# Output projection of tiles 0 to 7 in four pairs: seven products of halves and sums of halves, the fifth block of channels in plain products

## The chip, the core and the metric

The kernel runs on one core of a Trainium2 chip. The metric is the device time of one execution in microseconds, the median of several runs; lower is better. Five engines work side by side, each in its own program order: TensorE (PE, and PEld for its weight loads), VectorE (DVE), ScalarE (ACT), GpSimd (POOL) and SyncE (SP), which issues the DMAs here.

## The reference

A sequence of 2048 rows with 640 channels is normalized, goes through a sliding local attention with dilation (32 heads of 20 channels, 8 places at distance 2) and its output projection, and is gated by a bilinear feed-forward layer with 1536 hidden features:

```python
xn = _layernorm(x, axis=-1)
s = _A_ref(xn, A_wqkv, A_wo)             # attention, then @ wo
g = _silu(_B_ref(xn, B_w_gate, B_w_up, B_w_down))   # ((xn Wg) * (xn Wu)) Wd
return x + s * g
```

All matrix products have float32 inputs. The part that matters here is the last step of the attention, `o @ wo`: 2048 x 640 times 640 x 640.

## The kernel before

The 2048 rows lie in 16 tiles of 128. A product with float32 accuracy is made of three matmuls on TensorE: every operand is split into a high part `hi`, a copy on ScalarE in the type that TensorE multiplies quickly, and a low part `lo`, the operand less `hi`, made on VectorE or GpSimd (`split`, L83). `mm3` (L90) runs hi by hi over all blocks, then hi by lo, then lo by hi, into one PSUM bank.

The program runs in stages. The projections to queries, keys and values and the gate and up products (`gate_up`, L391) fill TensorE for the first 559 us, while VectorE does the attention (`attention`, L310) in small steps that `advance` and `drain` hand out. Each feature block `f` of the gate and up products runs over four chunks of 512 rows; the last two blocks are `f0` and `f1`. Then comes the output projection, 16 tiles of two column halves with 15 matmuls of 128x320 each (`out_proj`, L484), and at last the down products (`product`, L603).

The down products already use the scheme that the change brings to the output projection: two tiles make a pair, and the four quarters of the two-by-two product come out of seven products instead of eight (`W_IN`, `H_IN`, L497), with sums and differences of quarters as inputs. Three PSUM banks A, B, C serve them in the order A C A C A B A: a product with an old place accumulates on what the earlier one left, which ScalarE or VectorE must have read first (`gather`, L616). Quarter inputs for it are made ahead: `sum_wd` and `split_wd` (L517, L530) prepare the down weights during the output projection, one half block per tile.

Per tile the output projection takes these steps: `load_o` (L463) gathers the attention output from DRAM by four DMAs; `trans_o` (L472) turns the tile on VectorE in blocks of 32 by 32, copies `hi` on ScalarE and takes `lo` on VectorE; `out_proj` runs the 30 matmuls, and ScalarE copies each half to SBUF; one DMA stores the tile to `s_scr`. The tile of step s+1 is turned ahead of the matmuls of step s. The weight `wo` has five blocks of 128 channels, loaded and split behind the gate and up products (L775 to L788).

The order of each engine's work is the order of the program text. SBUF buffers go by tags with a fixed count of buffers (`st`, L75): a tile gets a buffer when the last reader of an earlier tile has finished. The tags of interest are `t` (two raw attention tiles of three), `wraw` (three raw weights), `wf` (four), `xc` (four: the normalized input, later down weights), `kv` (two: keys and values, later down weights) and `ot` (two turned tiles).

Of the kernel before, what the change touches and what calls it, by code (L numbers as in the profile page):

```python
# [19 lines left out]
P = 128  # L20
# [17 lines left out]
SCALE = DH ** -0.5  # L38
MASKED = -1e9 / SCALE
EPS = 1e-5  # L40
PAIRS = range(0, W, 2)
PACE = 1.0

# [7 lines left out]
def kernel(  # L51
# [23 lines left out]
    def st(shape, tag, bufs, dt=F32):  # L75
        cnt[0] += 1
        return sb.tile(shape, dt, tag=tag, bufs=bufs, name=f"{tag}_{cnt[0]}")

    def pt(shape, tag, bufs):
        cnt[0] += 1  # L80
        return ps.tile(shape, F32, tag=tag, bufs=bufs, name=f"{tag}_{cnt[0]}")

    def split(eng, raw, hi, lo):  # L83

        nc.scalar.activation(hi, raw, AF.Copy)  # L85
        eng.tensor_sub(lo, raw, hi.bitcast(F32))  # L86
# [3 lines left out]
    def mm3(acc, pairs, parts=ALL3, first=True, last=True):  # L90

        pairs = list(pairs)
        runs = [(a[i], b[j]) for i, j in parts for a, b in pairs]
        for n, (a, b) in enumerate(runs):
            nc.tensor.matmul(acc, a, b, start=first and n == 0, stop=last and n == len(runs) - 1)  # L95
# [376 lines left out]
    def trans_o(s):  # L472
        y = st([P, KD, P], "ot", 2)
        nc.vector.transpose(y.rearrange("p k (q i) -> p k q i", i=QB),
                            o_t.pop(s).rearrange("p (q k j) -> p k q j", q=NQ, j=QB))
        if s == NT - 2:
# [7 lines left out]
    def out_proj(s):  # L484
        a = oT.pop(s)
        y = st([P, D], "hs" if s % 2 and s < NT - 4 else "gs", 2)
        for n in range(2):
            c = slice(n * HALF, (n + 1) * HALF)
            p = pt([P, HALF], "q", 4)
            mm3(p, [([t[:, k, :] for t in a], [t[:, c] for t in wo_s[k]]) for k in range(KD)])  # L490
            nc.scalar.activation(y[:, c], p, AF.Copy)
        nc.sync.dma_start(s_scr[s], y)


    KH = KF // 2
# [4 lines left out]
    def begin_wd():  # L500

        big = [st([P, KH + 2, 2, HALF], "xc", NCH, F32R) for _ in range(4)]
        for name, y in zip(("B11", "T1", "T2", "B21"), big):
            wd_t[name] = [y[:, k] for k in range(KH)]
        wd_t["T3"] = [big[k // 2][:, KH + k % 2] for k in range(KH)]
        for name in ("B22", "T4"):
            y = st([P, KH, 2, HALF], "kv", 2, F32R)
            wd_t[name] = [y[:, k] for k in range(KH)]

    def load_wd(k):  # L510
        wd_raw[k] = st([P, 2, 2, HALF], "wraw", 3)
        for a in range(2):
            nc.sync.dma_start(wd_raw[k][:, a].rearrange("p a c -> p (a c)"), wd[:, a * KH + k, :])
# [126 lines left out]
        return lambda: None  # L640


    begin_unit(0)
    mask = st([1, NE, W], "mask", 1)
    nc.gpsimd.memset(mask, 0.0)
# [119 lines left out]
    for u in range(2, len(UN)):  # L765
        unit(u)
        for _ in range(3 + (u in (2, 5)) if u + 1 < len(UN) else len(pieces)):
            if len(pieces) == 1:
                load_wf(f1)
            piece()  # L770
    for ch in range(NCH):
        gate_up(f0, ch)
        if ch == 0:
            split_wf(f1, nc.gpsimd)
            load_wo((0, 1))  # L775
            load_wo((2, 3))
            t = load_wo((4,))
    for ch in range(NCH):
        if ch == 3:
            load_wd(0)  # L780
            trans_o(0)
            load_o(1, 1, st([P, 1, D], "o", 1))
            load_o(2, 3, st([P, 3, D], "t", 2))
            load_o(5, 3, st([P, 3, D], "t", 2))
        gate_up(f1, ch)
        if ch < 3:
            for k in ((0, 1), (2, 3), (4,))[ch]:
                split_wo(k)  # L788
        if ch == 1:
            drain(len(UN) - 2)  # L790
            load_o(0, 1, t[:, 1:2])
        if ch == 2:
            advance(1e9)

    load_wd(1)
    o_next = {3: (8, 3), 6: (11, 3), 9: (14, 2)}
    n_prod = 7 * NT // 2
    for s in range(NT):
        k, part = divmod(s - 1, 2)
        if s == 1:  # L800
            begin_wd()
        if s + 1 < NT:
            trans_o(s + 1)
        if s in o_next:
            load_o(*o_next[s], st([P, o_next[s][1], D], "t", 2))
        if 0 <= k < KH:
            sum_wd(k, part)
        out_proj(s)
        if 0 <= k < KH:
            split_wd(k, part)  # L810
            if part and k + 2 < KH:
                load_wd(k + 2)
        if s == 12:
            load_h(0)
        if s == 14:
            hi_h(0)
            lo_h(0)
# [72 lines left out]
```

## Time and profile before

| what | us |
|---|---|
| runs | 784.98, 783.54, 783.24 (median 783.54) |
| profiled execution | 783.21 |
| its span, first to last instruction | 781.4 |
| TensorE busy | 774.3 (99%) |
| VectorE busy | 667.2 (85%) |
| ScalarE busy | 230.9 (30%) |
| GpSimd busy | 135.8 (17%) |
| granted TensorE clock, mean | 0.999 |

The profile is that of one execution. Busy time is the time in which an engine has an instruction in work; matmuls are pipelined, so start-to-start distances say more of TensorE than durations. The "chain that ended last" follows the last instruction back to what released it, step by step. In groups and timelines the name left of the arrow is the tile that is written, those right of it are read; a group's row ends with the idle time of the engine ahead of its instructions and what ended it.

### The profile page before, as it was taken

Reading aid. Unit: us, or ns where it says so; the run is one execution under the profiler, and the core shown is the slowest. Engines: PE = TensorE matmul, PEld = TensorE weight load, DVE = VectorE, ACT = ScalarE, POOL = GpSimd, SP = SyncE. Lnnn points to the kernel's source line nnn. Section 1 sums busy time; section 2 is a strip of 40 time slices with the busy share of each in tenths; the row PEclk is TensorE's granted clock in tenths of the full one; section 3 lists DMA queues with packets and bytes.
Section 4 is the critical chain, followed back from the end, with each engine's and each line's share of the span. In section 5 each row is a group of like instructions: output and inputs, shape, how many; then the busy total and the mean of one; then the engine's idle time right before and its main releaser. Section 6 shows DMA issues by size and latency. Waiting matters only on the chain.

```text
span 781.4 us, 11205 instructions
## 1 busy us (share of the span) xinstructions
PE 774.3 (99%) x4432; PEld 706.1 (90%) x4432; DVE 667.2 (85%) x691; ACT 230.9 (30%) x527; POOL 135.8 (17%) x110
## 2 busy tenths in 40 slices
PE   8999999999999999999999999999999999999997
PEld 6989888898988898989898989888899999999997
DVE  6999898999999999996999998995368677777775
ACT  4323312031112121312131212112256554444442
POOL 5200401022013101210204001023177600000000
PEclk9999999999999999999999999999999999999999
DMA  9562131331224122423133131432967574555534
GB/s 330 161 198 75 43 96 38 96 90 48 84 49 124 49 64 81 119 61 79 29 99 92 39 105 39 129 100 70 242 186 217 167 263 156 198 192 183 182 101 136
DMA packets 82237, 93.99 MB, mean 120 GB/s; under 512 B 23096, under 2 KB 63368, under 8 KB 82056
## 3 DMA queue, kind: packets, MB, share of 16 engines
q1 hardware_dynamic: 82184, 93.27, 39.3%
q8 instruction: 35, 0.57, 0.3%
q14 instruction: 18, 0.15, 0.1%
HBM read 55.84 MB, written 28.31 MB: 108 GB/s over the span
## 4 chain that ended last, share of the span: by engine, by line
PE 99%; ACT 0%; DVE 0%; issue 0%; POOL 0%; POOLq 0%
PE q L299 27%; PE g L95 22%; PE u L95 22%; PE q L613 11%; PE q L95 9%; PE u L613 5%; PE g L613 3%; PE q L157 1%; PE q L223 0%; ACT xc L224 0%; PE g L223 0%; DVE q L599 0%; DVE q L600 0%; ACT q L594 0%; PE u L223 0%
## 5 line engine op out<-in xcount | busy, mean ns | idle before, releaser
L95 PE MATMUL g<-xc,wf 128*128 128x512 f32 (+1 forms) x735 | 176.4, 390 | 0.0
L95 PE MATMUL u<-xc,wf 128*128 128x512 f32 (+1 forms) x735 | 176.1, 390 | 0.0
L95 PEld LDWEIGHTS u<-xc,wf 128*128 128x128 f32 x735 | 135.7, 188 | 32.1
L95 PEld LDWEIGHTS g<-xc,wf 128*128 128x128 f32 x735 | 135.4, 188 | 31.1
L299 PE MATMUL q<-wqh,xc 128*128 128x300 f32 (+1 forms) x960 | 160.0, 310 | 0.9 <-ACT xc L224 0.9
L299 PEld LDWEIGHTS q<-wqh,xc 128*128 128x128 f32 x960 | 146.3, 188 | 2.8 <-ACT xc L224 1.3
L333 DVE TENSOR_TENSOR t<-q,kv 128x1600 f32<-128x1600 f32 (+1 forms) x48 | 96.9, 2018 | 9.1 <-DMA kv<-kv 9.1
L354 DVE TENSOR_TENSOR t<-e,kv 128x1600 f32<-128x1600 f32 (+1 forms) x48 | 97.6, 2050 | 1.1
L86 POOL TENSOR_TENSOR wf<-wraw,wf 128x256 fp32r<-128x256 f32 (+2 forms) x22 | 44.9, 2058 | 281.1 <-ACT wf L85 281.1
L336 DVE TENSOR_REDUCE lg<-t 128x80 f32<-128x1600 f32 (+1 forms) x48 | 92.6, 1929 | 1.1
L402 ACT ACTIVATE gs<-g 128x512 f32<-128x512 f32 x48 | 28.7, 597 | 213.9 <-PE g L95 208.7
L299 PE MATMUL q<-wql,xc 128*128 128x300 f32 (+1 forms) x480 | 86.2, 309 | 0.0
L301 ACT ACTIVATE kv<-q 128x200 f32<-128x200 f32 (+1 forms) x96 | 33.3, 347 | 144.9 <-PE q L299 144.9
L362 DVE TENSOR_TENSOR t<-t,t 128x1600 f32<-128x1600 f32 (+1 forms) x36 | 75.2, 2089 | 1.0
L299 PEld LDWEIGHTS q<-wql,xc 128*128 128x128 f32 x480 | 74.9, 188 | 0.0
L613 PE MATMUL q<-xc,wf 128*128 128x320 f32 x432 | 67.2, 308 | 0.0
L86 POOL TENSOR_TENSOR wql<-wraw,wqh 128x300 fp32r<-128x300 f32 (+4 forms) x15 | 36.1, 2431 | 168.3 <-ACT wqh L85 168.3
L613 PEld LDWEIGHTS q<-xc,wf 128*128 128x128 f32 x432 | 64.3, 188 | 0.0
L413 DVE TENSOR_TENSOR hs<-u,gs 128x512 f32<-128x512 f32 x47 | 32.1, 682 | 10.4 <-PE u L95 9.5
L95 PE MATMUL q<-wf,wf 128*128 128x320 f32 x156 | 35.1, 305 | 0.0
L86 DVE TENSOR_TENSOR wf<-ot,wf 128x640 fp32r<-128x640 f32 x13 | 15.0, 1156 | 20.0 <-ACT wf L85 17.1
L95 PEld LDWEIGHTS q<-wf,wf 128*128 128x128 f32 x156 | 26.0, 188 | 0.0
(170 smaller groups left out, 879.2 us busy)
## 6 DMA issues: line engine op xcount, KB each, us to landing
h_scr<-hs SPq DMA_DIRECT2D x48, 256.0 KB, 2.3
wraw<-in_wgu SPq DMA_DIRECT2D x12, 640.0 KB, 4.7
t<-h_scr SPq DMA_DIRECT2D x8, 768.0 KB, 7.8
hs<-s_scr SPq DMA_DIRECT2D x16, 320.0 KB, 3.9
gs<-in_x SPq DMA_DIRECT2D x16, 320.0 KB, 4.3
wraw<-h_scr SPq DMA_DIRECT2D x12, 384.0 KB, 6.2
out<-q SPq DMA_DIRECT2D x14, 320.0 KB, 2.6
wraw<-in_wd SPq DMA_DIRECT2D x12, 320.0 KB, 4.1
```

Source lines behind the costliest of these rows:

```text
L86: eng.tensor_sub(lo, raw, hi.bitcast(F32))
L95: nc.tensor.matmul(acc, a, b, start=first and n == 0, stop=last and n == len(runs) - 1)
L157: nc.tensor.matmul(pt([P, 3, P], "q", 4), ident, ident.unsqueeze(1).to_broadcast([P, 3, P]), start=True, stop=True)
L299: nc.tensor.matmul(p, xT[(r * NE + i) // TPC][a][:, k, t0:t0 + P], wq[g][b][:, k], start=n == 0, stop=n == len(runs) - 1, skip_group_check ...
L301: nc.scalar.activation(kv_t[u][:, :, W - 1 + i, :], p[:, c:].rearrange("p (a c) -> p a c", a=2), AF.Copy)
L333: nc.vector.tensor_mul(t, q.rearrange("p i c -> p (i c)").unsqueeze(1).to_broadcast([P, 2, NE * c]), places(0, j))
L336: nc.vector.tensor_reduce(out=lg[:, :, j:j + 2].rearrange("p n a -> p a n"), in_=heads(t), op=ALU.add, axis=AX.X)
L354: nc.vector.tensor_mul(heads(t), pw, heads(places(1, j)))
L362: nc.vector.tensor_add(acc, acc, t)
L402: nc.scalar.activation(gs, pp[0], AF.Copy)
L413: nc.vector.tensor_mul(hs, pp[1], gs)
L613: nc.tensor.matmul(p, y[:, i, k], wd_t[name][k][:, l], start=new and r == 0, stop=r == len(runs) - 1, skip_group_check=True)
```

## The change

Tiles 0 to 7 are taken in four pairs. With channels 0 to 255 and 256 to 511 as the two halves of the contraction and the two halves of the columns, each pair's quarters come out of seven products of two blocks each (six matmuls); the fifth block, channels 512 to 639, is added in plain products of three matmuls to the products that finish a quarter. Tiles 8 to 15 go as before.

What comes with it: the sums of quarters of `wo` are taken in place in its raw tiles and split into four more weights, held in parts of the `xc` buffers that the down weights fill later; the fifth block's difference of halves is one more. Each pair is loaded as one, turned, its sums taken (four on VectorE), and split in two parts of 768 and 1280 elements (`hi_pair` on ScalarE, `lo_pair` on VectorE) into parts of the `kv` and `xc` buffers or `wf`. The attention's remaining steps are handed out after the first chunk of `f1` instead of the third, the weights of blocks 2 and 3 are split a stage earlier, and the down weights are prepared at one half block per pair for the first three pairs, two for the fourth, then one per tile. The output tiles `y` are written by VectorE's additions as well as by ScalarE's copies.

```diff
     def trans_o(s):
-        y = st([P, KD, P], "ot", 2)
+        y = st([P, 2, KD, P], "ot", 2)[:, 0]
+        turn(y, s)
...
-            tag, n = ("kv", 2) if s == 0 else ("wf", 4) if s < NT - 2 else ("t", 2)
-            z = st([P, 2, KD, P], tag, n, F32R)
+            if s == SP:
+                z = blocks(wd_kv[0], 4, 2, KD)
...
+    def sums_wo():
+
+        r, u = wo_keep
+        b11, b12, b21, b22 = r[:, :, :HALF], r[:, :, HALF:], u[:, :, :HALF], u[:, :, HALF:]
+        nc.vector.tensor_sub(b11, b12, b11)
+        nc.vector.tensor_sub(b12, b22, b12)
+        nc.vector.tensor_sub(b22, b22, b11)
+        nc.vector.tensor_sub(b21, b21, b22)
+        wo_keep.append({"T1": b11, "T3": b12, "T2": b22, "T4": b21})
...
+    def split_t(name, y, r):
+        v = wo_keep[2][name]
+        t = y[:, r:r + KS]
+        split(nc.gpsimd, v, t[:, :, 0], t[:, :, 1])
+        wo_t[name] = [t[:, k] for k in range(KS)]
...
+    def load_pair(p):
+        t = st([P, 3, D], "t", 2)
+        load_o(2 * p, 2, t[:, 0:2])
...
+    def turn_pair(p):
+        y = pair_y[p] = st([P, 2, KD, P], "ot", 2)
+        for i in range(2):
+            turn(y[:, i], 2 * p + i)
+        s1, s2, s4 = (pair_raw[p][:, i] for i in range(3))
+        a11, a12, a21, a22 = (y[:, i, k:k + KS] for i in range(2) for k in (0, KS))
+        nc.vector.tensor_add(s1, a21, a22)
+        nc.vector.tensor_sub(s2, s1, a11)
+        nc.vector.tensor_sub(s4, a12, s2)
+        nc.vector.tensor_sub(a21, a11, a21)
+
+    def hi_pair(p, part):
...
+        nc.scalar.activation(z[0], raw, AF.Copy)
+
+    def lo_pair(p, part):
+        z, raw = pair_z[p, part]
+        nc.vector.tensor_sub(z[1], raw, z[0].bitcast(F32))
...
+    FIFTH = {3: ("a5", HALF), 4: ("b5", HALF), 5: ("a5", 0), 6: ("b5", None)}
+
+    def pair_product(p, j):
+        place = "ACACABA"[j]
+        new = j in (0, 1, 5)
...
+        runs = [(pair_in(p, H_IN[j], k, i), w_part(W_IN[j], k, l)) for i, l in ALL3 for k in range(KS)]
+        if j in FIFTH:
+            name, c = FIFTH[j]
+            runs += [(pair_in(p, name, 0, i), wo_t["W0-W1"][:, l] if c is None else wo_s[KD - 1][l][:, c:c + HALF])
+                     for i, l in ALL3]
...
+        kept, (ya, yb) = pair_k[0], y_t.setdefault((p, "y"), [None, None])
+        if j < 3:
+            nc.scalar.activation(kept[:, j], b, AF.Copy)
+        elif j == 3:
+            ya = y_t[p, "y"][0] = st([P, D], "gs", 2)
+            nc.vector.tensor_add(ya[:, HALF:], kept[:, 2], b)
+        elif j == 4:
+            yb = y_t[p, "y"][1] = st([P, D], "hs", 2)
+            nc.vector.tensor_add(yb[:, HALF:], kept[:, 1], b)
+        elif j == 5:
+            nc.vector.tensor_add(ya[:, :HALF], kept[:, 0], b)
+            nc.sync.dma_start(s_scr[2 * p], ya)
+        else:
+            nc.scalar.activation(yb[:, :HALF], b, AF.Copy)
+            nc.sync.dma_start(s_scr[2 * p + 1], yb)
...
+        elif ch < 3:
+            split_wo(ch + 1)
+    gate_up(f1, 0)
+    advance(1e9)
+    split_wo(0)
+    split_wo(1)
+    load_pair(0)
+    load_pair(1)
+    begin_wd(kv=True)
+    begin_wd()
+    gate_up(f1, 1)
+    split_wo(4)
+    sums_wo()
+    wo_keep.append(w5)
+    split_t("T1", wd_big[0], 4)
+    split_t("T2", wd_big[0], 6)
+    turn_pair(0)
+    hi_pair(0, 0)
+    hi_pair(0, 1)
+    begin_wd()
+    gate_up(f1, 2)
+    sum_w5()
+    split_w5()
+    lo_pair(0, 0)
+    lo_pair(0, 1)
+    split_t("T3", wd_big[1], 4)
+    split_t("T4", wd_big[1], 6)
+    load_pair(2)
+    load_wd(0)
     load_wd(1)
...
+    turn_pair(1)
+    begin_wd()
+    gate_up(f1, 3)
+    begin_wd()
+    hi_pair(1, 0)
+    sum_wd(0, 0)
+    split_wd(0, 0)
+    turn_pair(2)
...
+    pair_product(0, 0)
+    for p in range(SP // 2):
+        more = p + 1 < SP // 2
+        n = 1 + (p > 2)
+        if more:
+            lo_pair(p + 1, 0)
+        pair_product(p, 1)
+        wd_sums(n)
+        pair_product(p, 2)
+        if more:
+            hi_pair(p + 1, 1)
+        pair_product(p, 3)
+        wd_splits(n)
+        pair_product(p, 4)
+        if more:
+            lo_pair(p + 1, 1)
+        else:
+            trans_o(SP)
+        pair_product(p, 5)
+        if p == 0:
+            load_pair(3)
+        elif p == 1:
+            turn_pair(3)
+            load_o(SP, 3, st([P, 3, D], "t", 2))
+        elif p == 2:
+            load_o(SP + 3, 3, st([P, 3, D], "t", 2))
+        if more:
+            pair_product(p + 1, 0)
+        else:
+            out_proj(SP, 0)
+        pair_product(p, 6)
+        if p + 2 < SP // 2:
+            hi_pair(p + 2, 0)
```

`turn` is the transpose that stood in `trans_o`, `blocks` a view of a part of a buffer as operand blocks, and `wd_sums` and `wd_splits` walk through the half blocks of the down weights; `begin_wd` gives out its buffers one at a time.

More of the change, by code (lines that the diff above doesn't have):

```diff
@@ L498, with begin_wd, blocks @@
     H_IN = ("A11", "S1", "S2", "S4", "S3", "A12", "A22")
[L500 to L508, printed above, removed]
+    wd_big, wd_kv = [], []
+    def begin_wd(kv=False):
+        if kv:
+            for name in ("B22", "T4"):
+                y = st([P, KH, 2, HALF], "kv", 2, F32R)
+                wd_kv.append(y)
+                wd_t[name] = [y[:, k] for k in range(KH)]
+            return
+        y = st([P, KH + 2, 2, HALF], "xc", NCH, F32R)
+        wd_t[("B11", "T1", "T2", "B21")[len(wd_big)]] = [y[:, k] for k in range(KH)]
+        wd_big.append(y)
+        if len(wd_big) == NCH:
+            wd_t["T3"] = [wd_big[b][:, k] for b, k in ((2, 6), (2, 7), (3, 7), (3, 6), (1, 6), (1, 7))]
+    def blocks(y, r, h, n):
+        return y[:, r:].rearrange("p r i c -> p (r i c)")[:, :h * n * P].rearrange("p (h n c) -> p h n c", h=h, c=P)
     def load_wd(k):
@@ new lines, in split_t, with split_w5, w_part @@
+    def split_t(name, y, r):
[3 more added lines that the diff above has]
+        wo_t[name] = [t[:, k] for k in range(KS)]
+    def split_w5():
+        t = wd_kv[1][:, KH - 1]
+        split(nc.gpsimd, wo_keep[3][:, :HALF], t[:, 0], t[:, 1])
+        wo_t["W0-W1"] = t
+    def w_part(name, k, l):
+        if name in wo_t:
+            return wo_t[name][k][:, l]
+        a, c = divmod(int(name[1:]) - 11, 10)
+        return wo_s[a * KS + k][l][:, c * HALF:(c + 1) * HALF]
@@ new lines, in hi_pair @@
+    def hi_pair(p, part):
+        if part == 0:
+            if p % 2:
+                z = [st([P, 2, KD, P], "wf", 4, F32R).rearrange("p a k c -> p (a k) c")[:, :3 * KS] for _ in range(2)]
+            else:
+                z = blocks(wd_kv[1], 2, 2, 3 * KS)
+                z = [z[:, 0], z[:, 1]]
+            raw = pair_raw[p].rearrange("p a k c -> p (a k) c")
+        else:
+            z = blocks(wd_big[3], 3, 2, 2 * KD) if p % 2 else blocks(wd_kv[0], 2, 2, 2 * KD)
+            z = [z[:, 0], z[:, 1]]
+            raw = pair_y[p].rearrange("p a k c -> p (a k) c")
+        pair_z[p, part] = z, raw
+        nc.scalar.activation(z[0], raw, AF.Copy)
@@ L812 @@
                 load_wd(k + 2)
+        del wd_steps[:n]
+    pair_product(0, 0)
[14 more added lines that the diff above has]
+            lo_pair(p + 1, 1)
+        else:
+            trans_o(SP)
[9 more added lines that the diff above has]
+            pair_product(p + 1, 0)
+        else:
+            out_proj(SP, 0)
+        pair_product(p, 6)
+        if p + 2 < SP // 2:
+            hi_pair(p + 2, 0)
+    n_prod = 7 * NT // 2
+    for s in range(SP, NT):
+        if s + 1 < NT:
+            trans_o(s + 1)
+        if s == SP + 2:
+            load_o(SP + 6, 2, st([P, 2, D], "t", 2))
+        wd_sums(1)
+        if s > SP:
+            out_proj(s, 0)
+        out_proj(s, 1)
+        wd_splits(1)
         if s == 12:
```

84 lines of the change are left out of this document (42 added, 42 removed).

## The prediction

> **What bounds the kernel now.** I read the page first: the span, the chain that ended last, then the stage that the change rebuilds, as one stretch of the windows view (after the engine columns: granted clock, DMA share, GB/s).
>
> ```profile
> span 781.4 us, 11205 instructions
> PE 99%; ACT 0%; DVE 0%; issue 0%; POOL 0%; POOLq 0%
> core 0: us, PE busy (x) PEld busy (x) DVE busy (x) ACT busy (x) POOL busy (x), PEclk, DMA share, GB/s
> 559.20:629.30 70.10, 70.10 (x483) 70.08 (x482) 46.92 (x55) 39.17 (x90) 42.35 (x43) 1.00 0.66 191
> ```
>
> The chain is TensorE from start to end, and in the output projection (559.20 to 629.30) TensorE has no gap, at full clock, while VectorE has a third of its time free. So a matmul less is worth its start-to-start time, and a wait that stops TensorE for 1 us costs 1 us. The timeline and the chain in order of time give that distance:
>
> ```profile
> 559.21 0.46 PE L95 MATMUL q<-wf,kv 128*128 128x320 f32 x2
> ...
> 629.28 2.64 PE q L613 x18
> ```
>
> The stage has 16 tiles of 30 matmuls, 480 in 70.07 us: 0.146 us each.
>
> The change's new steps are priced by these groups (line, engine, output<-inputs, shapes, count | busy, mean ns):
>
> ```profile
> L572 ACT ACTIVATE wf<-wqh 128x768 fp32r<-128x768 f32 x16 | 13.6, 849 | 19.2 <-PE q L613 8.9 <-PE g L613 8.6 <-DVE wf L576 1.3
> L85 ACT ACTIVATE wf<-wraw 128x1280 fp32r<-128x1280 f32 x1 | 1.3, 1264 | 0.0
> L474 DVE STREAM_TRANSPOSE ot<-t 128x640 f32<-128x640 f32 x14 | 11.7, 833 | 0.0
> L86 DVE TENSOR_TENSOR t<-ot,t 128x640 fp32r<-128x640 f32 x1 | 0.8, 824 | 0.8 <-ACT t L85 0.8
> L576 DVE TENSOR_TENSOR wf<-t,wf 128x768 fp32r<-128x768 f32 x16 | 15.3, 956 | 8.5 <-ACT wf L572 7.8
> L522 DVE TENSOR_TENSOR lg<-wraw 128x320 f32<-128x320 f32 x6 | 6.3, 1046 | 0.0
> L523 DVE TENSOR_TENSOR lg<-wraw,lg 128x320 f32<-128x320 f32 x6 | 6.4, 1063 | 0.5
> L527 DVE TENSOR_TENSOR wraw<-wraw 128x320 f32<-128x320 f32 x6 | 3.6, 599 | 0.0
> L528 DVE TENSOR_TENSOR e<-wraw,lg 128x320 f32<-128x320 f32 x6 | 2.9, 483 | 0.0
> L629 DVE TENSOR_TENSOR q<-e,u 128x320 f32<-128x320 f32 x8 | 3.9, 487 | 3.8 <-PE u L613 3.8
> L86 POOL TENSOR_TENSOR xc<-wraw,xc 128x320 fp32r<-128x320 f32 x18 | 15.8, 879 | 18.6 <-ACT xc L85 18.6
> L86 POOL TENSOR_TENSOR wql<-wraw,wql 128x640 fp32r<-128x640 f32 x1 | 1.6, 1571 | 0.0
> ```
>
> From 640 to 768 elements VectorE needs 132 ns more, 1.03 ns an element; so 256 elements take about 0.42 us and 1280 about 1.48 us. Four VectorE lines of one form, 128x320, lie between 483 and 1063 ns. The timeline shows why (start, duration):
>
> ```profile
> 576.58 1.16 DVE L522 TENSOR_TENSOR lg<-wraw 128x320 f32<-128x320 f32 x1
> 577.83 1.19 DVE L523 TENSOR_TENSOR lg<-wraw,lg 128x320 f32<-128x320 f32 x1
> ...
> 577.79 0.88 POOL L86 TENSOR_TENSOR xc<-wraw,xc 128x320 fp32r<-128x320 f32 x1 [0.40 <-ACT xc L85]
> 578.62 1.13 POOL L86 TENSOR_TENSOR kv<-wraw,kv 128x320 fp32r<-128x320 f32 x1
> ```
>
> L523 comes while GpSimd has just started; it ends 0.4 us after GpSimd's operation, and GpSimd's next one is longer by 0.25. The two take turns: a VectorE operation on two SBUF operands waits for the GpSimd operation in flight. The mean extra over L522, L523, L527 and L528 is (1046+1063+599+483)/4 - 483 = 315 ns.
>
> **Removed.** A pair of tiles was 60 matmuls. It becomes six for each of seven products plus four plain fifth-block groups of three: 54. Four pairs save 24 x 0.146 = 3.5 us. Shape and type stay, so the pace should.
>
> **The preparation, beside the gate and up products.** Sums of the weights (four of 640 elements), their splits, two pairs of turned and summed inputs and the loads go ahead of 559.21. There the helpers have room (the bracket is the idle time before):
>
> ```profile
> 538.47 0.69 DVE L413 TENSOR_TENSOR hs<-u,gs 128x512 f32<-128x512 f32 x1 [3.00 <-PE u L95]
> 545.47 0.69 DVE L413 TENSOR_TENSOR hs<-u,gs 128x512 f32<-128x512 f32 x1 [6.31 <-PE u L95]
> 543.22 1.57 POOL L86 TENSOR_TENSOR wqh<-wraw,wqh 128x640 fp32r<-128x640 f32 x1 [3.91 <-ACT wqh L85]
> t<-o_scr SPq DMA_DIRECT2D x4, 160.0 KB, 4.7
> wraw<-in_wd SPq DMA_DIRECT2D x12, 320.0 KB, 4.1
> ```
>
> SyncE issues the first pair's four loads behind the last attention store, so they land by 542 to 546. The weight sums end near 542.3. Turning pair 0 takes two transposes and four sums, 3.3 us, and takes turns with GpSimd's splits of block 4, T1 and T2: near 549.2. The hi copies follow on ScalarE to 550.9, ahead of a gate copy that was ready 2 us earlier; its bank is wanted again only in the new stage, so this lateness is free. The lo halves end near 552.5, 6.7 us before TensorE needs them: cost nothing, and if that cover went each late us would count in full. GpSimd ends T3 near 554.9; only then has the first down weight its buffer, and its second load, issued 0.45 us later, lands 4.1 us on, about 559.4. This wait stands in SyncE's queue; behind it are only the other down weight and a store with buffers to spare. Pair 1 is turned by 557.9. Moving the splits of blocks 2 and 3 a stage earlier delays attention by at most a GpSimd operation each, 2 x 1.57 us, against the 3.00 idle: nothing. The loads of the attention output stay 28, the stores of the result 16, of the same bytes in all.
>
> **Waits that the new stage adds.** Products now last 0.88 us (6) or 1.31 us (9), and they accumulate over the bank that the product two before them left, so its copy must be finished first. Each engine works in program order. I follow that order from these rows:
>
> ```profile
> 559.41 0.60 ACT L415 ACTIVATE hs<-u 128x512 f32<-128x512 f32 x1 [2.83 <-PE u L95]
> 559.90 0.73 ACT L85 ACTIVATE wf<-ot 128x640 fp32r<-128x640 f32 x1
> 561.67 0.44 ACT L491 ACTIVATE gs<-q 128x320 f32<-128x320 f32 x1 [1.04 <-PE q L95]
> 568.53 0.46 ACT L85 ACTIVATE xc<-wraw 128x320 fp32r<-128x320 f32 x1
> 568.88 0.46 ACT L85 ACTIVATE kv<-wraw 128x320 fp32r<-128x320 f32 x1
> 630.01 0.96 DVE L562 TENSOR_TENSOR wqh<-wqh,wraw 128x768 f32<-128x768 f32 x1
> 630.89 0.96 DVE L576 TENSOR_TENSOR wf<-wqh,wf 128x768 fp32r<-128x768 f32 x1
> ```
>
> ScalarE's next operation starts 0.1 us before the end of the last, VectorE's 0.08; ScalarE's L491 starts 0.27 us after TensorE issued 15 matmuls (559.21 + 2.19 = 561.40).
>
> (a) *First copy.* Behind the last gate-up product ScalarE has in order: that product's copy (559.41), the 768-element hi of pair 1 (whose buffer is also free only then; 0.75), three hi copies of the down weight (3 x 0.36), and only then the copy of the first product: 559.90 + 0.75 + 1.08 = 561.73, done 562.17. Product three could start at 559.21 + 12 x 0.146 = 560.96: **+1.2 us**. With the down weight after 560.7 it grows one for one; I bound it at 1.2 and 2.4.
>
> (b) *Pair 0 to pair 1.* Pair 1's first product needs the lo of its last inputs. After the down weight VectorE has: two sums (0.8), turning pair 2 (2.8), lo 768 (0.87), two sums (0.8), two additions out of the banks, the second after product five, lo 1280 (1.48). Undelayed: 563.0 after turning, 564.7 before the additions; product five is issued by 565.73 with (a), its addition done at 566.4, the lo at 567.9. TensorE wants it four matmuls into pair 1, at 567.6: 0.3. GpSimd has meanwhile seven split operations, and eight of these VectorE operations read two SBUF operands. At 315 ns each, 0.9 us of it absorbed before product five's addition: 0.3 + 7 x 0.315 - 0.9 + 0.315 = 1.9. Strictly by turns, operation by operation, the lo ends at 570.9: 3.3. The rows are nearer to turns, but the mean is what turns came to over a stage: I take the middle, **+2.6** (0.3 to 3.3).
>
> [...]
>
> (c) *Pairs 1 to 2 and 2 to 3.* The lo cannot start before the addition of product five: 0.27 + 0.40 + 1.48 = 2.15 us and 0.05 for the signal, while TensorE has product six (1.31) and four matmuls (0.58): 0.3, plus 0.3 for one turn with GpSimd: **+0.6 each, 1.2** (0.6 to 2.0).
>
> (d) *Copy behind pair 3's hi.* Turning pair 3 begins after those same steps, and the hi of pair 3 stands ahead of the copy of pair 2's second product. Counted from the end of pair 1's fifth product: additions and lo 2.48, two transposes 3.98, three sums 5.05, hi and copy to 6.29, against 5.56 when product four of pair 2 could start: **+0.8** (0.5 to 1.6). The hi of pair 2 has the same place a pair earlier without that wait: **+0.1**.
>
> (e) *From pair 3 to tile 8.* Its turn stands behind product five's addition: 0.27 + 0.40 + 0.83 + 0.1 + 0.73 + 0.05 = 2.4 us, against product six, 1.31: **+1.1** (1.0 to 1.4).
>
> **After the pairs** eight tiles run as before. The down weights end one tile (4.4 us) later, and the third load for the down products waits for the buffer that this split reads:
>
> ```profile
> 618.71 0.88 POOL L86 TENSOR_TENSOR xc<-wraw,xc 128x320 fp32r<-128x320 f32 x1
> wraw<-h_scr SPq DMA_DIRECT2D x3, 384.0 KB, 4.2
> ```
>
> It was issued near 619.6, 9.7 us before the stage ended; now 5.3 us, and 4.2 to landing leaves 1.1: nothing, up to 1.0 if it is late.
>
> **The sum.** -3.5 + 1.2 + 2.6 + 1.2 + 0.8 + 0.1 + 1.1 = +3.5 us. The profiled execution took 783.21 us, 781.4 of span and 1.8 around it; it lies 0.3 under the median of 783.54. So 786.7 beside the profile, **787.0** beside the median. The least waits add to 3.7 and the greatest to 10.8, which spans 783.7 to 790.8; the foot of that is the first rival below, and the forecast's own range is 784.7 to 790.
>
> **Rivals.** About 0.2%, 1.6 us, is what a measurement can tell from no change.
>
> *Turns cost nothing.* GpSimd has fewer splits per microsecond than before, so VectorE may miss it each time. Left: 1.2 + 0.3 + 0.6 + 0.8 + 0.1 + 1.1 = 4.1, +0.6: 784.1. Against it: the splits follow a product's additions, just where the lo stands.
>
> *Faster: the lo halves keep ahead.* If VectorE reaches each lo before TensorE arrives, (b), (c) and (d) vanish and (a) and (e) remain: -3.5 + 2.3 = -1.2, 782.3; with a ScalarE entry that also hides (a), 781.1. For it: a third of VectorE is idle in the stage, and each wait of TensorE gives the helpers time. It decides where the lo is done within 1.9 us of product five's end. Against: the order on VectorE puts that addition ahead, so 2.2 us is the least.
>
> *One long wait halves the clock.* TensorE's last matmuls are at 774.28 to 777.08, then:
>
> ```profile
> 774.28 2.80 PE L613 MATMUL q<-kv,wf 128*128 128x320 f32 x18
> ...
> 779.00:780.00 1.00, 0.00 (x0) 0.00 (x0) 0.00 (x0) 0.00 (x0) 0.00 (x0) 0.76 0.46 164
> 780.00:781.40 1.40, 0.00 (x0) 0.00 (x0) 0.00 (x0) 0.00 (x0) 0.00 (x0) 0.50 0.00 0
> ```
>
> A mean of 0.76 is half clock from 779.5: 2.4 us after the last matmul. If (b) is 3.3 or the down weight is late, the clock falls; if it takes as long to return, 2.4 us run at half pace and cost 1.2 more: 787 + 0.7 + 1.2 and up, 789 to 791.
>
> [...] No run here shows the return.
>
> **How the numbers follow.** Forecast (slower by the sum) 0.55; turns free 0.18; faster 0.12; half clock or late load 0.15. Slower by over 0.2%: 0.55 + 0.15 = 0.70; within: 0.18; faster: 0.12. Low end 781.8, between the two figures of the faster case, high end 790.5: about 0.08 lie outside on each side.
>
> **What would show it.** For (a): TensorE idle near 561 to 562.2, released by ScalarE's copy of the first product. For (b) and (c): gaps before pairs 1, 2 and 3, released by VectorE's 1280-element lo, and VectorE's 256-element sums above 0.42 us where GpSimd splits. For (d): a gap in pair 2 behind a ScalarE copy; for (e): one before tile 8, released by a ScalarE hi. The 54 matmuls a pair and 0.146 us are checked in the same stage. I am wrong if TensorE shows less than 2 us of idle time there, or if the gaps stand before 559 or after tile 8.

## The result and the profile after

| | before | after |
|---|---|---|
| median of the runs, us | 783.39 (4 runs: 782.98 to 784.98) | 790.39 (4 runs: 788.88 to 792.27) |
| profiled execution, us | 783.21 | 789.44 |
| its span, us | 781.4 | 787.7 |

The changed kernel takes 1.0089 times the time of the one before (95% interval 1.0075 to 1.0103): 7.0 us more by the medians, 6.3 us by the profiled spans. The page says in its fourth part where the end comes from now:

```profile
span 787.7 us, 11213 instructions
...
PE 87%; DVE 6%; issue 2%; POOL 2%; DMA 1%; ACT 1%; SPq 0%; POOLq 0%; DVEq 0%; ACTq 0%
```

The chain was 99% TensorE; now 6% of it lies on VectorE, 2% on GpSimd and 1% on DMAs. These shares are larger than the waits: from the matmul that waits at 570.4 the chain goes back along VectorE and its loads to about 510 us, through the end of the attention, most of which ran beside a TensorE without a gap. The windows view puts a number on the stage: 47.10 us from its start, the same length in both kernels, first after, then before (span, PE busy (matmul records), PEld, DVE, ACT, POOL, granted clock).

```profile
558.90:606.00 47.10, 40.89 (x268) 39.13 (x267) 34.18 (x49) 25.08 (x53) 25.34 (x25) 1.00 0.60 174
```

```profile
559.20:606.30 47.10, 47.10 (x325) 47.09 (x324) 33.27 (x38) 26.82 (x63) 31.12 (x32) 1.00 0.77 211
```

TensorE, which had no gap, stands still for 6.2 of the 47.1 us, at full clock. The timeline of TensorE names each gap. A row is start, duration, line, tiles, count; the bracket is the idle time before it and what ended it.

```profile
558.91 1.04 PE L755 MATMUL q<-wf,kv 128*128 128x320 f32 x6
...
561.89 1.15 PE L755 MATMUL q<-xc,kv 128*128 128x320 f32 x6 [0.99 <-ACT o L758]
...
570.40 0.56 PE L755 MATMUL q<-wf,xc 128*128 128x320 f32 x2 [2.82 <-DVE xc L734]
570.80 1.04 PE L755 MATMUL q<-xc,kv 128*128 128x320 f32 x6
...
579.30 0.56 PE L755 MATMUL q<-wf,kv 128*128 128x320 f32 x2 [0.62 <-DVE kv L734]
583.76 0.41 PE L755 MATMUL u<-wqh,kv 128*128 128x320 f32 x1 [0.82 <-ACT o L758]
588.75 0.56 PE L755 MATMUL q<-wf,xc 128*128 128x320 f32 x2 [0.18 <-DVE xc L734]
597.15 0.56 PE L96 MATMUL q<-wf,kv 128*128 128x320 f32 x2 [0.78 <-ACT kv L86]
...
637.44 2.90 PE L633 MATMUL u<-xc,wf 128*128 128x320 f32 x18 [1.04 <-ACT wf L592]
640.50 2.91 PE L633 MATMUL q<-xc,wf 128*128 128x320 f32 x18 [0.16 <-ACT lg L610]
```

The first row with a bracket is (a) of the prediction (the copy of the first product), the next (b) (the lo of pair 1), 579.30 and 588.75 are (c), 583.76 is (d), 597.15 is (e) (the first tile outside the pairs). The last two stand in the down products, after tile 8, where the prediction had nothing.

Read as starts against the pace of 0.146 us, the gaps are: (a) third product at 561.89, due 12 matmuls after 558.91 at 560.66, 1.23 us; (b) 2.98; (c) 0.79 and 0.33; (d) 0.99, and 0.1 a pair earlier; (e) 0.95. Together 7.4. Six matmuls behind a wait take 1.15 us where six in the stream take 1.04, so each restart costs 0.1 more, some 0.65 over the stage. Less the 3.5 us of the removed matmuls that is +4.5 by tile 8. The waits in the down products bring 1.6 and small delays there 0.5, which no experiment takes apart; the stage began 0.3 earlier. The sum is the 6.3 us between the spans.

All kernels below are compared by two stretches: *pairs*, from the first matmul of the stage to the first of tile 8, when nine matmuls of the pairs are still to come, and *rest*, from there to the end of the span. For the kernel before, the same work is 231 matmuls, 33.7 us, and 781.4 - 559.2 - 33.7 = 188.5.

| kernel | median (runs) | ratio to before, interval | pairs | rest |
|---|---|---|---|---|
| before | 783.2 to 783.4 | 1 | 33.7 | 188.5 |
| after | 790.39 (4) | 1.0089 (1.0075, 1.0103) | 38.2 | 190.6 |
| load_later | 790.04 (4) | 1.0083 (1.0063, 1.0102) | 39.8 | 188.8 |
| copy_first | 791.95 (4) | 1.0106 (1.0090, 1.0121) | 40.9 | 190.0 |
| splits_later | 791.38 (4) | 1.0103 (1.0087, 1.0118) | 35.5 | 194.6 |
| lo_ahead | 787.30 (4) | 1.0049 (1.0034, 1.0064) | 35.8 | 190.3 |
| turn_later | 787.79 (4) | 1.0056 (1.0042, 1.0070) | 36.6 | 189.5 |
| fill_wait | 788.64 (6) | 1.0067 (1.0054, 1.0079) | 38.2 | 189.6 |
| all_but_loads | 783.30 (11) | 1.0000 (0.9992, 1.0009) | 31.8 | 189.7 |
| all_in_order | 781.87 (11) | 0.9981 (0.9972, 0.9990) | 31.8 | 188.9 |

The longest wait, (b), is not a long operation but a queue of short ones. VectorE in the changed kernel, from the sums of pair 2 to the lo that TensorE waits for:

```profile
561.39 0.97 DVE L712 TENSOR_TENSOR t<-t,ot 128x256 f32<-128x256 f32 x1
562.39 0.99 DVE L713 TENSOR_TENSOR t<-ot,t 128x256 f32<-128x256 f32 x1
563.31 1.10 DVE L714 TENSOR_TENSOR ot<-ot 128x256 f32<-128x256 f32 x1
...
567.78 0.47 DVE L764 TENSOR_TENSOR hs<-o,q 128x320 f32<-128x320 f32 x1
568.18 2.17 DVE L734 TENSOR_TENSOR xc<-ot,xc 128x1280 fp32r<-128x1280 f32 x1
```

GpSimd beside it:

```profile
561.03 1.05 POOL L87 TENSOR_TENSOR xc<-wraw,xc 128x320 fp32r<-128x320 f32 x1
562.04 1.06 POOL L87 TENSOR_TENSOR kv<-wraw,kv 128x320 fp32r<-128x320 f32 x1
563.06 1.07 POOL L87 TENSOR_TENSOR xc<-lg,xc 128x320 fp32r<-128x320 f32 x1
...
567.07 1.11 POOL L87 TENSOR_TENSOR xc<-wraw,xc 128x320 fp32r<-128x320 f32 x1
```

VectorE's ends and GpSimd's interlock: 562.36 and 562.08, 563.38 and 563.10, 564.41 and 564.13. Both engines advance by about one operation per 1.0 us, although VectorE's sum alone takes 0.42 (splits_later, below). The operations that suffer here, these sums at 0.97 to 1.10 us, have two SBUF operands; the addition at 567.78 reads a PSUM bank and takes 0.47, no more than that at 570.27 with GpSimd quiet, beside the GpSimd split that starts at 567.07. The timeline shows no idle time of VectorE from 557.64 to 570.7.

The waits after tile 8 begin in SyncE's queue. In it, issues of one group stand as one row, and the duration includes the time that the queue waited for a buffer:

```profile
621.10 0.32 SPq L502 DMA_DIRECT2D s_scr<-gs  x1
621.52 7.27 SPq L571 DMA_DIRECT2D wraw<-h_scr  x3
628.84 0.42 SPq L571 DMA_DIRECT2D o<-h_scr  x1
629.32 7.69 SPq L502 DMA_DIRECT2D s_scr<-gs  x3
```

The loads for the down products stand ahead of the stores of tiles 13 and later. The third load waits for its buffer and holds the queue for 7.27 us; the stores wait behind it, and the output buffers that they read are not free. ScalarE pays for that, with everything behind the copy:

```profile
629.68 0.84 ACT L592 ACTIVATE wf<-wraw 128x768 fp32r<-128x768 f32 x1
635.89 0.77 ACT L499 ACTIVATE gs<-q 128x320 f32<-128x320 f32 x2 [5.37 <-DMA s_scr<-gs]
636.54 1.58 ACT L592 ACTIVATE wf<-wqh 128x768 fp32r<-128x768 f32 x2
```

Tile 15's copies wait 5.37 us for a store of an earlier tile, and the hi that the second down product needs comes behind them. What TensorE loses by it is not the same each time: in all_but_loads, which leaves these loads where they are, ScalarE waits 4.46 us at this place, and in the profiles of the kernels below that leave them there TensorE's listed wait at the second down product is anything from none (turn_later, fill_wait) to 0.69 us (lo_ahead).

### The profile page after: what moved, and what is told of

Same layout as the page of the kernel before. It is cut to its first block, busy times and chain, and to the rows that moved or that the text cites. A ratio compares the mean times of both kernels' runs of the same rounds, so it can differ in the third digit from the quotient of the medians.

```text
span 787.7 us, 11213 instructions
## 1 busy us (share of the span) xinstructions
PE 773.5 (98%) x4408; PEld 703.0 (89%) x4408; DVE 691.1 (88%) x724; ACT 236.4 (30%) x532; POOL 147.3 (19%) x115
## 4 chain that ended last, share of the span: by engine, by line
PE 87%; DVE 6%; issue 2%; POOL 2%; DMA 1%; ACT 1%; SPq 0%; POOLq 0%; DVEq 0%; ACTq 0%
PE q L300 27%; PE u L96 18%; PE g L96 18%; PE q L633 10%; PE u L633 5%; PE g L633 3%; PE q L755 2%; PE q L96 2%; PE u L755 1%; POOL xc L87 1%; DMA s_scr<-gs 1%; DVE t L363 1%; DVE ot L474 1%; POOL kv L87 1%; PE q L158 1%
## 5 line engine op out<-in xcount | busy, mean ns | idle before, releaser
L87 POOL TENSOR_TENSOR wf<-wraw,wf 128x256 fp32r<-128x256 f32 (+2 forms) x22 | 47.9, 2196 | 269.4 <-ACT wf L86 269.4
L87 POOL TENSOR_TENSOR wql<-wraw,wqh 128x300 fp32r<-128x300 f32 (+4 forms) x15 | 34.1, 2295 | 168.4 <-ACT wqh L86 168.4
L87 POOL TENSOR_TENSOR xc<-wraw,xc 128x320 fp32r<-128x320 f32 (+1 forms) x22 | 24.6, 1120 | 25.9 <-ACT xc L86 18.3
L303 ACT ACTIVATE q<-q 128x100 f32<-128x100 f32 (+1 forms) x96 | 24.6, 256 | 0.0
L633 PE MATMUL u<-xc,wf 128*128 128x320 f32 x144 | 22.5, 309 | 1.0 <-ACT wf L592 1.0
```

Of the source, the lines that this page charges most:

```text
L303: nc.scalar.activation(q_t[u][:, i, :], p[:, :c], AF.Copy)
L633: nc.tensor.matmul(p, y[:, i, k], wd_t[name][k][:, l], start=new and r == 0, stop=r == len(runs) - 1, skip_group_check=True)
```

## The experiments

The theory: every gap in the pairs is a helper's place in its program order, (a) and (d) on ScalarE, (b) on VectorE with GpSimd's turns, (c) and (e) on VectorE; the gap in the down products is the load in SyncE's queue; and the executions that take longer than the profiled one lose it to a fall of the granted clock. The rivals are a shortage of VectorE or GpSimd as such, so that no order helps, and a price of the new matmuls themselves.

### load_later: the loads for the down products one tile later

```diff
-        if s == 12:
+        if s == 13:
             load_h(0)
```

> The first four loads for the down products are issued one tile later (behind the splits of tile 13 instead of tile 12), so SyncE no longer stands before the store of tile 13's output while it waits for GpSimd's last split. Theory (the store behind a waiting load is what is late): the waits of TensorE at the second and third down product (1.04 and 0.16 us in the changed kernel's profile) fall under 0.3 us together, the copies of tile 15 on ScalarE no longer wait for a store, and the time falls by 1.2 to 1.9 us. Rival (the third load's own landing is late, whatever stands behind it): the wait moves to VectorE's sum of that load and the time stays within 0.4 us. Nothing in the pairs changes.

SyncE in this kernel:

```profile
622.88 4.68 SPq L502 DMA_DIRECT2D s_scr<-gs  x2
627.66 3.56 SPq L571 DMA_DIRECT2D wraw<-h_scr  x3
```

The stores go first, the copies of tile 15 no longer wait for one, and both waits in the down products are gone: the rest takes 188.8 us instead of 190.6. The median hardly moved, 790.04 against 790.39. The windows view tells why:

```profile
570.00:571.00 1.00, 0.34 (x2) 0.34 (x3) 1.00 (x2) 0.00 (x0) 0.00 (x0) 1.00 0.00 0
571.00:572.00 1.00, 1.00 (x6) 1.00 (x5) 0.00 (x1) 0.44 (x1) 0.00 (x0) 0.60 0.24 70
...
573.00:574.00 1.00, 1.00 (x6) 1.00 (x5) 0.00 (x0) 0.43 (x2) 0.00 (x0) 0.50 0.44 132
574.00:575.00 1.00, 1.00 (x7) 1.00 (x6) 0.23 (x1) 0.74 (x2) 0.00 (x0) 0.69 0.45 113
```

The third column from the right is the granted clock. After the same wait (b), 2.87 us here, the clock fell to half from 571.2 to 574.6, 3.4 us in which half the matmuls run; the pairs take 39.8 instead of 38.2 us. The gain behind tile 8 was there, and a loss of 1.6 us in the pairs hid it, with 0.2 of a later start of the stage. The mechanism stands by the trace, the price of 1.8 us by this one profile; the pair of kernels at the end measures it again.

### copy_first: the first down weight split behind the copies of pair 0

```diff
-    split_wd(0, 0)
     turn_pair(2)
...
         pair_product(p, 1)
+        if p == 0:
+            split_wd(0, 0)
```

> The three splits of the first half block of the down weights stand behind the copy of pair 0's second product on ScalarE instead of ahead of the copy of the first. The wait (a) before the third product of pair 0 (1.23 us in the changed kernel's profile) falls to about 0.2 us in any case. Theory (the pairs' entry is one chain through VectorE, which works without a pause up to the last lo half of pair 1, so (a) only pays part of (b) in advance): the wait before pair 1 grows from 2.98 to about 4.0 us, the time stays within 0.4 us, or rises by 1 to 2 us if so long a wait halves the granted clock. Rival (the two waits are independent): the wait before pair 1 stays near 3.0 and the time falls by 1.0 us.

(a) is gone, and all of it came back in (b):

```profile
570.84 0.90 PE L755 MATMUL q<-wf,xc 128*128 128x320 f32 x2 [4.15 <-DVE xc L734]
```

TensorE arrives 0.9 us earlier at a lo that ends 0.4 later, so the wait is 1.3 longer. VectorE works without a pause ahead of that lo, so TensorE doesn't hold it up; (a) alone cost nothing as long as (b) stood behind it. In this profile the clock fell in the longer wait, for twice as long as in load_later; the median is 1.6 us above that of the changed kernel, though the intervals of the two overlap:

```profile
565.00:570.00 5.00, 1.69 (x12) 1.43 (x10) 5.00 (x6) 0.94 (x2) 4.44 (x4) 0.94 0.05 18
570.00:575.00 5.00, 4.16 (x15) 4.16 (x16) 1.19 (x2) 1.26 (x3) 0.00 (x0) 0.50 0.36 107
575.00:580.00 5.00, 5.00 (x32) 5.00 (x32) 2.79 (x6) 3.46 (x7) 0.98 (x2) 0.88 0.53 160
```

Half clock from 569.4 to 576.2, 6.8 us.

### splits_later: GpSimd's splits moved out of pair 0

```diff
-    split_wd(0, 0)
     turn_pair(2)
...
-        n = 1 + (p > 2)
+        n = (1, 0, 1, 1)[p]
...
-        wd_splits(n)
+        if p:
+            wd_splits(n)
...
+        if p == 0:
+            split_wd(0, 0)
+            wd_splits(1)
         pair_product(p, 6)
...
-        wd_sums(1)
+        wd_sums(1 + (s < SP + 2))
...
-        wd_splits(1)
+        wd_splits(1 + (s < SP + 2))
```

> GpSimd's seven splits of the first down-weight block (and their hi copies) wait until pair 1's first product; the sums on VectorE stay where they are, and the later half blocks are spread anew (none in pair 1's loop, one each in pairs 2 and 3, two each in tiles 8 and 9). Theory (turns with GpSimd make the wait before pair 1): VectorE's two-operand sums between 559 and 567 fall to 0.42 and 0.48 us but for the one behind the last gate-up product's multiplication, the last lo of pair 1 takes 1.5 instead of 2.2 us and ends near 566.5, and the wait before pair 1 falls from 2.98 to 0.3 to 0.6 us; (a) falls from 1.23 to 0.2 with it; the time falls by 3 to 4 us less what later turns give back, up to 1 us. Rival (VectorE's own work makes it): the operations do not shorten, the wait before pair 1 and (a) add to 3 us or more and the time falls by no more than 1 us.

VectorE, the same operations as above:

```profile
561.48 0.42 DVE L712 TENSOR_TENSOR t<-t,ot 128x256 f32<-128x256 f32 x1
...
565.13 1.49 DVE L734 TENSOR_TENSOR xc<-ot,xc 128x1280 fp32r<-128x1280 f32 x1
```

With GpSimd quiet the sums take 0.42 instead of 0.97 to 1.10 and the lo 1.49 instead of 2.17; it ends at 566.6, and of the 2.98 us ahead of pair 1 some 0.3 are left, too little for the timeline to list. So with VectorE's operations and their order as they were, the turns with GpSimd make most of (b). But the splits have to be somewhere, and I had the price of that too low. TensorE in the same kernel:

```profile
571.71 0.41 PE L755 MATMUL u<-wqh,wf 128*128 128x320 f32 x1 [1.39 <-ACT o L758]
...
611.74 0.56 PE L96 MATMUL q<-wf,wf 128*128 128x320 f32 x2 [2.57 <-ACT wf L86]
```

Seven hi copies in a row now stand ahead of pair 1's copies on ScalarE, and the sums of two half blocks in tile 9, drawn out to 1.00 to 1.17 us each beside GpSimd, delay the turn of tile 11; there the clock fell as well (0.77 and 0.89 in the two 5 us stretches from 610). The pairs take 35.5 us, 2.7 less, and the rest 4.0 more.

### lo_ahead: VectorE's order in pairs 1 to 3

```diff
-        if more:
-            lo_pair(p + 1, 0)
+        if p == 0:
+            lo_pair(1, 0)
         pair_product(p, 1)
...
         if more:
+            if p:
+                hi_pair(p + 1, 0)
             hi_pair(p + 1, 1)
+        else:
+            trans_o(SP)
...
-        pair_product(p, 4)
         if more:
             lo_pair(p + 1, 1)
-        else:
-            trans_o(SP)
+        pair_product(p, 4)
+        if p and more:
+            lo_pair(p + 1, 0)
...
-        if p + 2 < SP // 2:
-            hi_pair(p + 2, 0)
```

> On VectorE the 1280-element lo halves of pairs 1 to 3 stand ahead of the addition of the fifth product, tile 8 is turned ahead of the fourth product of pair 3, and the 768-element hi and lo of pairs 2 and 3 stand behind the copies of the products that they blocked. Theory (the order on VectorE and ScalarE makes the waits before pairs 2, 3 and tile 8 and the one behind pair 3's hi): the waits of 0.79, 0.33, 0.99 and 0.95 us, with 0.1 us for each new start, vanish to under 0.5 together; (a) and the wait before pair 1 stay at 1.2 and 2.2 to 3.0; the time falls by 2.5 to 3.5 us. Rival (these waits are turns with GpSimd or lack of time on VectorE, not order): at least half of the 3.1 us comes back and the time falls by less than 1.5 us.

(c), (d) and (e) are gone from the timeline of TensorE; (a) stays, and (b) is shorter, as its lo now passes one addition and itself takes 1.75 instead of 2.17 us:

```profile
562.50 1.15 PE L755 MATMUL q<-xc,kv 128*128 128x320 f32 x6 [0.99 <-ACT o L758]
570.21 0.90 PE L755 MATMUL q<-wf,xc 128*128 128x320 f32 x2 [2.01 <-DVE xc L734]
```

The kernel takes 3.1 us less than the one after the change (787.30 against 790.39), with the same work on the same engines in another order. In the profiled execution the clock fell even so, for 3.4 us and thus about 1.7 us of time, behind a shorter wait than in load_later or copy_first:

```profile
568.00:569.00 1.00, 0.20 (x2) 0.00 (x0) 1.00 (x3) 0.47 (x1) 1.00 (x2) 1.00 0.00 0
...
570.00:571.00 1.00, 0.79 (x3) 0.79 (x4) 1.00 (x4) 0.00 (x0) 0.88 (x1) 0.59 0.00 0
```

### turn_later: pair 2 turned behind the lo of pair 1

```diff
-    turn_pair(2)
...
         pair_product(p, 5)
         if p == 0:
+            turn_pair(2)
             load_pair(3)
```

> Only the turning and the four sums of pair 2 move on VectorE: from ahead of pair 0's products to behind the addition of pair 0's sixth product. Theory (the wait before pair 1 is what stood ahead of pair 1's last lo on VectorE): that wait falls from 2.98 us to under 1.0; (a) stays at 1.2; pair 2's hi on ScalarE, which stands ahead of the copy of pair 1's second product, now waits for the turning, so a wait of 1 to 2 us appears before the fourth product of pair 1, as (d) does in pair 2; sum of TensorE's idle time in the pairs 1 us lower at most, the granted clock more often whole, time 1 to 2.5 us lower. Rival (turns with GpSimd alone hold that lo, wherever pair 2 is turned): the wait before pair 1 stays above 2 us.

```profile
568.97 0.57 PE L755 MATMUL q<-wf,xc 128*128 128x320 f32 x2 [0.67 <-DVE xc L734]
573.43 0.42 PE L755 MATMUL u<-wqh,wf 128*128 128x320 f32 x1 [0.81 <-ACT o L758]
```

(b) falls from 2.82 to 0.67 with GpSimd's splits left where they were, and one new wait of the size of (d) takes a part back. No execution of this kernel shows a fall of the clock: all four have a mean of 0.999 or 1.0, and they lie within 1.2 us where those of the changed kernel lie within 3.4.

### fill_wait: the wait of (b) filled with matmuls

```diff
+        if p == 0:
+            b = pt([P, HALF], "q", 4)
+            for _ in range(18):
+                nc.tensor.matmul(b, pair_in(0, "A11", 0, 0), w_part("B11", 0, 0), start=True, stop=True)
         if more:
             pair_product(p + 1, 0)
```

The 18 matmuls write a bank that nobody reads.

> The changed kernel with 18 more matmuls (2.6 us of TensorE), whose result nobody reads, between pair 0's sixth product and pair 1's first: they fill the long wait (2.98 us) and lengthen nothing behind it by more than 0.3 us. Theory (part of the loss, and the spread of the changed kernel's runs from 788.9 to 792.3, is the clock that halves in or after the long wait in some executions): the granted clock is 1.00 in the stretch from 565 to 580, all runs lie between 788.7 and 789.9 and the median falls by 0.8 to 1.5 us to about 789.2. Rival (the spread has another cause): median and spread as they were, 790.4 and 3 us, or higher by what the matmuls cost.

TensorE has 18 matmuls more in the time of (b), and pair 1 goes on when it did:

```profile
566.84 2.81 PE L989 MATMUL q<-wf,kv 128*128 128x320 f32 x18
569.48 0.75 PE L755 MATMUL q<-wf,xc 128*128 128x320 f32 x4
570.43 0.41 PE L755 MATMUL q<-wf,xc 128*128 128x320 f32 x1 [0.20 <-DVE xc L734]
```

The pairs take 38.2 us in both profiles. The six executions lie between 788.35 and 789.06, all at a mean clock of 0.999 or 1.0. Of the changed kernel's four, the two at 1.0 took 788.88 and 789.44, and those at 0.998 and 0.994 took 791.35 and 792.27. So the two executions with a lower clock took 2.2 and 3.1 us more than the mean of the others, 789.16; these two were not profiled, so where in them the clock fell was not seen. Of the 1.75 us between the medians 1.2 are that (790.39 less 789.16). The other 0.5, which makes the gain larger than expected, fits the rest, 189.6 against 190.6 us, as this kernel's profile lacks the listed wait at the second down product.

### all_in_order and all_but_loads: what the seven products are worth

all_in_order puts together lo_ahead, load_later and turn_later, and splits the first down weight behind `hi_pair(1, 1)`; all_but_loads is the same with the loads for the down products at tile 12.

```diff
-    split_wd(0, 0)
-    turn_pair(2)
...
             hi_pair(p + 1, 1)
+            if p == 0:
+                split_wd(0, 0)
...
         if p == 0:
+            turn_pair(2)
             load_pair(3)
```

> Four moves at once: lo halves, tile 8 and the hi of pairs 2 and 3 as in the run lo_ahead, the loads of the down products as in load_later, pair 2 turned as in turn_later, and the first three splits of the down weights behind the hi of pair 1's second part on ScalarE. Theory (all of the loss is order and the clock that falls in the long wait; the products themselves save 3.5 us): TensorE's waits in the stage add to under 1.0 us, the granted clock stays 1.0 through it, and the time is 780 to 781.5 us, 2 to 3.5 us under the kernel before. Rival (VectorE and GpSimd have not the time in the pairs, so a wait removed comes back at another place, as in splits_later): waits of 3 us or more remain and the time is 784 us or above.

One wait is left in TensorE's timeline behind 559 in all_in_order:

```profile
575.12 0.56 PE L755 MATMUL q<-wf,kv 128*128 128x320 f32 x2 [0.33 <-DVE kv L734]
```

The median is 781.87 us, 1.4 less than the kernel before in the same comparison (783.30); the ratio is 0.9981 (0.9972 to 0.9990). The pairs take 31.8 us, 1.9 less than in the kernel before, and the rest 0.4 more. It is a little slower than I had expected, since of the 3.5 us of the removed matmuls 1.6 are still lost in the pairs, 0.6 of it in the wait above with its restart, and 0.5 and 0.3 in two places (ahead of 583.88 and 561.16) where matmuls start a few tenths late without the timeline counting a wait. The granted clock is 1.00 through the stage; the mean of 0.998 in this execution comes from a fall near 777.5, after the last matmul.

> The kernel all_in_order with the first loads of the down products put back to tile 12, where the change has them. Theory (SyncE stands in its queue before the store of tile 13, and tile 15's copies wait for that store): waits of TensorE of 1.0 to 1.5 us at the second and third down product come back, the copies of tile 15 on ScalarE wait over 3 us for a store, and the time is 1.2 to 1.9 us above all_in_order, 783.1 to 783.8. Rival (with the pairs mended the store has time enough): no wait there and the time within 0.4 us of all_in_order.

Against it, all_but_loads shows the price of the loads with no fall of the clock in the way: 783.30 (11 runs), 1.4 us more and no different from the kernel before (783.16). The profiles show 0.9 of it behind tile 8 (189.7 against 188.9) and 0.2 as a later start of the stage. ScalarE has its mark again. The waits of 1.0 to 1.5 us that I expected on TensorE did not come back in this profile: by the starts the second down product is 0.29 us late and the third 0.43, and only the third is listed:

```profile
629.23 0.77 ACT L499 ACTIVATE gs<-q 128x320 f32<-128x320 f32 x2 [4.46 <-DMA s_scr<-gs]
```

```profile
633.85 2.91 PE L633 MATMUL q<-xc,wf 128*128 128x320 f32 x18 [0.16 <-ACT lg L610]
```

## Why the prediction was right, and where not

*The saving.* 24 matmuls at 0.146 us are the 3.5 us of the forecast: with the waits and restarts taken off, the stage after runs at the pace of before. The most that an order here kept of it is 1.9 us in the pairs (all_in_order).

*(a), forecast 1.2.* Measured 1.23. The ScalarE queue was read rightly, row by row: the hi of pair 1, three hi copies, then the copy. But copy_first shows that it had no price of its own. The lo of (b) comes at a time that VectorE and GpSimd set between them, so (a) only moves a part of (b) ahead; I had put the two into one sum, which gave the right total because (b) was worked out with (a) in it.

*(b), forecast 2.6 between 0.3 and 3.3.* Measured 2.98, near the upper end, the one with strict turns. I had taken the middle because four lines averaged to 315 ns extra over the stage of before. Here they came back to back with GpSimd's queue full, and the three sums shown above took 0.97 to 1.10 us instead of 0.42. The ends of both engines, 0.28 us apart three times running, fit the turns taken operation by operation. splits_later, which took GpSimd's operations away, and turn_later, which took four sums and two transposes away, shrink the wait from either side, to 0.3 and 0.8 us by the starts. So it takes both, the turns and the length of VectorE's queue ahead of the lo.

*(c), forecast 1.2.* Measured 0.79 and 0.33, 1.12. *(d), forecast 0.8 and 0.1.* Measured 0.99 and 0.1. *(e), forecast 1.1.* Measured 0.95. lo_ahead shows that all three hang on VectorE's and ScalarE's order: with the lo ahead of the additions they vanish, though no engine does less. The first (c) has a turn with GpSimd in it besides: its lo took 2.03 us, that of the second 1.59, which makes nearly all of the 0.46 between the two waits.

*Left out: the restart.* The sum took each wait as the distance to the release. A stream that stops also starts up again, 0.1 us each time, and six waits made 0.65 us of it.

*Luck.* The waits of the pairs add to 7.4 us where the forecast had 7.0, but it is a sum of errors of both signs, and the largest term, (b), was the middle between two ways of counting of which one was borne out.

*The step that failed: "nothing, up to 1.0 if it is late".* After the pairs I asked only when the third load for the down products would land. That was read rightly: it was issued 5.1 us before the first down product, where I had 5.3, and in load_later, where it comes only 4.5 us before, nothing waits. What cost 1.6 us in the profile (1.8 by the rest of load_later) was behind it: three stores in SyncE's queue, whose buffers ScalarE wanted, whose next hi copies TensorE wanted. I had listed what is queued behind the other waiting loads, not behind this one. load_later removes the wait; between all_in_order and all_but_loads the place of the loads is worth 1.4 us by the medians, 1.1 of it visible in the profiles. The prediction would have called a gap after tile 8 a sign of error, and there was one.

*The rival of the half clock.* The forecast's mechanism decided, and yet the rival was a part of it. The profiled execution kept full clock; two of the four executions didn't, which puts the median 0.95 above the profile, where I had added 0.3. By its number alone, 789 to 791, this rival fits the median of 790.39 better than the forecast does; but the profiled execution, without a fall, has 6.3 of the 7.0 us, and those are the waits. The 2.4 us that I had read from the end of the profile are no firm bound: the clock fell after 2.0 us in lo_ahead and did not fall in the 2.82 us of the changed kernel's profile. Nor did the clock return after 2.4 us, as the rival took it: half clock lasted 3.4 us in load_later and lo_ahead, so 1.7 us of time by estimate, and 6.8 in copy_first.

*The other rivals.* "Turns cost nothing" falls by the DVE rows. "The lo halves keep ahead" does not happen in the order as it was changed; in the order of lo_ahead and all_in_order it does, and there the kernel is faster. So the seven products lose here by the order around them.

*The size.* The kernel is 7.0 us slower where 3.5 were forecast, twice as much. The median lies 0.4 above the forecast's own range (784.7 to 790) and only 0.1 inside the high end of 790.5. So the kind and the place of the waits in the pairs were right, and the total was not. The forecast of 787.0 lies 3.4 us under the median: 0.4 for the waits in the pairs, 0.65 for restarts, 2.1 behind tile 8 and 0.65 for the clock, less 0.3 for the earlier start of the stage.

## What to carry over

Where one engine runs without a gap, work taken from it can turn into waits for the helpers' queues, as here (7.4 us of waits where 3.5 were saved): follow each helper's program order past the removed work, and put what the next step needs ahead of what only has to be done sometime. Waits in a row on one chain aren't a sum; removing the first may only lengthen the second. When a wait appears in a DMA queue, as the 7.27 us in SyncE's here, look at the stores behind it and at who wants their buffers.

## What the hardware showed that I had not expected

The clock's fall didn't go by the length of the wait alone. It fell 2.0 us after the last matmul had ended (lo_ahead, at 570.2), 2.7 us after (copy_first, at 569.4), and 3.4 us after, when matmuls ran again for half a microsecond (load_later, at 571.2); in the changed kernel's profile it didn't fall at all, with nearly the same wait, 2.82 us:

```profile
570.00:571.00 1.00, 0.60 (x4) 0.60 (x5) 0.74 (x2) 0.00 (x0) 0.00 (x0) 1.00 0.00 0
571.00:572.00 1.00, 1.00 (x9) 1.00 (x8) 0.00 (x0) 0.44 (x1) 0.00 (x0) 1.00 0.47 152
```

Each time it stayed at half for 3.4 us (in splits_later too) or, in copy_first, for 6.8, twice that; there TensorE still stood for the first 1.4 us of the fall. A wait of 2.01 us came ahead of a fall in lo_ahead, and one of 2.82 us stayed without any in the changed kernel's profile; no run here shows what besides the wait decides it, so that stays open.
